# A spectral layer and two MLP layers on one core: rounding of weights in five steps, the mix's split ahead of the threshold, first inverse results in other PSUM banks

## Chip, core, metric

The kernel runs on one core of a Trainium2 chip. The metric is the device time of one launch in microseconds, lower is better. Engines: PE is TensorE, DVE is VectorE, ACT is ScalarE, POOL is GpSimd, SP is the SyncE queue that issues most DMAs.

## What is computed

```python
X = np.fft.rfft(x, axis=1)                   # x: 2 x 3008 x 256
Yr = Xr @ w_r - Xi @ w_i + b_r
Yi = Xr @ w_i + Xi @ w_r + b_i
Yr = np.sign(Yr) * np.maximum(np.abs(Yr) - 0.01, 0.0)   # Yi alike
y = np.fft.irfft(Y, n=3008, axis=1)
h = y.reshape(6016, 256) @ w_in1             # 256 x 2048
z = (h / (1 + exp(-h))) @ w_out1             # 2048 x 256
out = leaky(z @ w_in2) @ w_out2              # maximum(0.01 * h, h)
```

## The kernel before, in words

Every float32 product is made of three passes over parts: a number is split into a high part `hi` (rounded to the format fp32r by a conversion) and a low part `lo` (the difference). So each result that is to be multiplied again costs a copy on ACT (`hi`) and a subtraction on DVE or POOL (`lo`).

The program is one long list in a manual schedule: each engine runs its instructions in the order in which the Python code issues them. It has four stretches. The first transform of length 47 comes first (until about 34 us; `pa`, L276). Then comes the **spectrum**: 48 items, one per frequency row and batch. Then the inverse transform of length 47 (`inverse`, `px`, L424) and the first MLP layer start, interleaved, and the second layer follows.

An item j passes through eight parts. The list `STAGES` (L377) gives their order within one call `spectrum(j)` and the lag of each, so `spectrum(j)` runs `threshold` of item j-3, `split_z` of j-1, `split_y` of j-3, `seed` of j-1, `store` of j-5, `mix` of j, `forward` of j-2 and `backward` of j-4:

- `mix` (L321, PE): six matmuls of 512 columns into `pz`, one of the two banks of `ps_a[0]`.
- `split_z` (L330, L331): ACT copies `pz` to `zh`, DVE subtracts to `zl`. After that the bank is free.
- `seed` (L336, DVE): copies the bias into a bank `py` of `ps_h` (four banks).
- `forward` (L344, PE): six matmuls of 256 columns onto `py`.
- `threshold` (L350, L351): ACT makes `cy` from `py`, DVE then finishes `cy` in place.
- `split_y` (L358, L359): ACT copies `cy` to `yh`; `yl` is subtracted by DVE for even item numbers (so in `spectrum(j)` with odd j) and by POOL for the others.
- `backward` (L367, PE): three matmuls of 256 columns into `pb`, one of the two banks of `ps_a[1]`.
- `store` (L373, L374): ACT copies `pb` to `bo`, SP sends it to memory.

Behind these, `split_dm` splits the transform table of item j+1 (`dmh` by ACT or POOL in turn, L238; `dml` by POOL, L239), and `load_dm` loads that of j+4. In the first 28 items a table serves two items.

Behind each `spectrum(j)` stands `fifth_w(i)`, with i = j % 5 for the first 28 items and (j - 28) % 3 after that. It rounds the first layer's weights piece by piece for later use. `begin` makes `wc` and `wm` on ACT (L138, L140), then two DVE instructions on `wm` (L143, L145); `scale` is one DVE instruction (L150); `around` is an addition on POOL (L157), and with it goes the load of a further piece by SP (L131); `split` is a copy on ACT (L164) and a subtraction on POOL (L165). Splits in this stretch stop at 16 pieces. Before the change, i = 0 or 3 splits one piece and begins another, i = 1 or 4 scales, i = 2 or 4 adds and loads. Inside the MLP layers `step_w` goes on with the rest.

At the end of the loop two groups of the inverse transform are made, with two tiles `px` each (h = 0 and 1): both of the first group, then `spectrum(48)`, then both of the second, then `spectrum(49)`. Each `px` is split by ACT (`xhi`, L431) and DVE (`xlo`, L432). Before the change, h = 0 takes a bank of `ps_a[0]`, h = 1 one of `ps_h`. `spectrum(50)` to `spectrum(52)` run between the first matmuls of the MLP (`ph`, L520, in `ps_h`).

Of the kernel before, what the change touches and what calls it, by code (L numbers as in the profile page):

```python
# [76 lines left out]
def spectral_mlp_kernel(ctx, tc, x, w_r, w_i, b_r, b_i, w_in1, w_out1, w_in2, w_out2, da, ea, dm, out):  # L77
# [3 lines left out]
    def pool(name, bufs, stack=ctx, **kw):  # L81
        return stack.enter_context(tc.tile_pool(name=name, bufs=bufs, **kw))
# [4 lines left out]
    ps_h = pool("ps_h", 4, space=bass.MemoryType.PSUM)  # L87
    ps_a = [pool(f"ps_a{i}", 2, space=bass.MemoryType.PSUM) for i in range(2)]
# [20 lines left out]
    def weight_pieces(win, wout, in_dst, out_dst, n_dst, first=0):  # L109

        win, wout = win.bitcast(U32), wout.bitcast(U32)
        pieces = []
        for q in range(NF // 2 + 1):
            new = []
            if q < NF // 2:
                for d in range(2):
                    new.append((win[d * 128:(d + 1) * 128, q * 512:(q + 1) * 512], lambda d=d, q=q: [w[:, d, q % 4 * 256:][:, :256] for w in in_dst(q // 4)]))  # L120
            if q:
                for f in (2 * q - 2, 2 * q - 1):
                    new.append((wout[f * 128:(f + 1) * 128, :], lambda f=f: [w[:, f % HALF * D:][:, :D] for w in out_dst(f // HALF)]))
            pieces += new[2:] + new[:2] if q == 4 else new
        loaded, begun, scaled, rounded, made = [], [], [], [], []

        def load():
            if pieces:
                src, dst = pieces.pop(0)
                raw = raws[0].tile([128, 512], F32, tag="wraw", name="wraw", bufs=4 if raws[1:] else 2).bitcast(U32)  # L130
                nc.sync.dma_start(out=raw, in_=src)  # L131
                loaded.append((raw.rearrange("p (e w) -> p e w", w=2), dst))

        def begin():
            raw, dst = loaded.pop(0)
            m = stage.tile([128, 256], U32, tag="wm", name="wm", bufs=2)
            c = stage.tile([128, 256], F32, tag="wc", name="wc", bufs=4).bitcast(U32)
            nc.scalar.activation(out=c, in_=raw[:, :, 0], func=ACTF.Copy, scale=2.0 ** -29)  # L138

            nc.scalar.activation(out=m.bitcast(F32), in_=raw[:, :, 1].bitcast(F32), func=ACTF.Copy, scale=2.0 ** -112)  # L140
            yield

            nc.vector.tensor_scalar(out=m.bitcast(F32), in0=m.bitcast(F32), scalar1=MAG, scalar2=-MAG, op0=ALU.min, op1=ALU.max)  # L143
            yield
            nc.vector.tensor_scalar(out=m, in0=m, scalar1=3, scalar2=0x7FFFFFFF, op0=ALU.logical_shift_left, op1=ALU.bitwise_and)  # L145
            begun.append((raw, m, c, dst))

        def scale():
            raw, m, c, dst = begun.pop(0)
            nc.vector.scalar_tensor_tensor(out=m, in0=raw[:, :, 1], scalar=0x80000000, in1=m, op0=ALU.bitwise_and, op1=ALU.bitwise_or)  # L150
            yield
            scaled.append((m, c, dst))

        def around(add):
            m, c, dst = scaled.pop(0)
            r = dst()[0].bitcast(U32) if n_dst == 1 else c
            add.tensor_tensor(out=r, in0=c, in1=m, op=ALU.add)  # L157
            rounded.append((c.bitcast(F32), dst))

        def split():  # L160
            c, dst = rounded.pop(0)
            if n_dst == 2:
                hi, lo = dst()
                nc.scalar.copy(hi, c)  # L164
                nc.gpsimd.tensor_tensor(out=lo, in0=c, in1=hi.bitcast(F32), op=ALU.subtract)  # L165
            made.append(1)

        def step():

            if scaled:  # L170
                around(nc.gpsimd)
            parts = [p() for p, ready in ((scale, begun), (begin, loaded and len(begun) < 2)) if ready]
            done = len(rounded)
            while parts:
                for p in list(parts):
                    if next(p, parts) is parts:
                        parts.remove(p)
            for _ in range(done):
                split()
            if scaled:  # L180
                around(nc.gpsimd)
            load()

        def fifth(i):

            if i in (0, 3):
                if rounded and len(made) < first:
                    split()
                if loaded and not begun:
                    list(begin())  # L190
            elif i in (1, 4) and begun:
                list(scale())
            if i in (2, 4) and scaled:
                around(nc.gpsimd)
                load()

        def until(n):
            while len(made) < min(n, 2 * NF):
                step()

        return load, step, fifth, until

    raws = [stage]
    load_w, step_w, fifth_w, until_w = weight_pieces(
        w_in1, w_out1, lambda k: [w_in[k][p] for p in parts], lambda k: [w_out[k][p] for p in parts], 2, NF)

# [167 lines left out]
        nc.sync.dma_start(out=scr[4 * k:4 * k + 4, b], in_=bo)  # L374


    STAGES = [(threshold, 3), (split_z, 1), (split_y, 3), (seed, 1), (store, 5), (mix, 0), (forward, 2), (backward, 4)]  # L377

    def spectrum(j):
        for part, lag in STAGES:  # L380
            if 0 <= j - lag < len(items):
                part(j - lag)
        split_dm(j + 1)
        load_dm(j + 4)
# [4 lines left out]
    def load_b():  # L389
        if groups:  # L390
            g, n = groups.pop(0)
            b, p = divmod(g, R2 // 2)
            bt = btp.tile([NJ, NG, D], F32, tag="bt", name="bt")
            nc.sync.dma_start(out=bt[:, :n], in_=scr[:, b, p:p + n, :])
            bts.append((g, n, bt))
# [21 lines left out]
    def inverse(h, c):  # L417

        g, n, bt = bts[0]

        at_, tag = (ps_a[1], "acc") if c in (1, 2) else (ps_a[0], "acc") if c == h == 0 else (ps_h, "h")
        px = at_.tile([128, 512], F32, tag=tag, name="px")
        for s in range(n):
            nc.tensor.matmul(px[:, s * PAIR:(s + 1) * PAIR], lhsT=bt[:, s, h * 128:(h + 1) * 128],  # L424
                             rhs=ea_sb, start=True, stop=True, skip_group_check=True)
        t0, t1 = g * PAIR, (g + n) * PAIR
        cut = min(t1, t0 + RING - at(t0))
        for a, b in ((t0, cut), (cut, t1)):
            if a < b:
                hi, lo = (r[:, h, at(a):at(a) + b - a] for r in ring)  # L430
                nc.scalar.copy(hi, px[:, a - t0:b - t0])  # L431
                nc.vector.tensor_tensor(out=lo, in0=px[:, a - t0:b - t0], in1=hi.bitcast(F32), op=ALU.subtract)  # L432
        if h == 1:
            bts.pop(0)
            load_b()
# [13 lines left out]
    made = [0]  # L449

    def ahead(layer, c):

        if layer == 2:
            return [lambda: load_x2(c), None] + [lambda h=h: split_x2(c, h) for h in range(2)]
        steps = []
        while made[0] < sum(CHUNKS[c]):
            made[0] += sizes.pop(0) * PAIR
            steps += [lambda h=h: inverse(h, c) for h in range(2)]
        return steps
# [220 lines left out]
    for i in range(len(pairs) + 2):  # L680
# [70 lines left out]
        if k <= i <= NF:  # L751
            split_w()
            if i < NF:
                sums_w1(i - k)
        elif i < tail:
            if i == NF + 1:
                for home in homes:
                    m_in.append(home.tile([128, DFF], F32, tag="hold0", name="m_in").rearrange("p (d c) -> p d c", d=2))
                    m_out.append(home.tile([128, DFF], F32, tag="hold1", name="m_out"))
                _, step_w, _, _ = weight_pieces(w_in2, w_out2, lambda k: [m_in[k]], lambda k: [m_out[k]], 1)  # L760
            if i > NF and i % 2 == 0:
                step_w()
        else:
            split_w()
            if i - tail in IN_AT:
                next_in(IN_AT.index(i - tail))
            if i - tail in SUMS_AT:
                sums_w2(SUMS_AT.index(i - tail))
# [27 lines left out]
```

## Time and profile before

| | |
|---|---|
| median of 3 runs | 1165.65 us (1165.25 to 1167.86) |
| the profiled execution, whole | 1165.78 us |
| its span, first to last instruction | 1164.0 us |
| PE busy | 1154.2 us (99%) |
| DVE, ACT, POOL busy | 711.3 (61%), 764.3 (66%), 592.0 us (51%) |
| mean granted clock of PE | 1.000 of full speed |

The span is 1.78 us shorter than the execution. Times in the rows are microseconds from the start of the span unless marked ns; a row of the timeline gives start, duration, engine, line, operation, output and inputs, and in brackets the idle time before it with what ended it. Instructions of one engine overlap a little, so the distance from start to start is less than the duration. PE's float32 matmuls are recorded as two each.

### The profile page before, as it was taken

The page shows a single profiled execution, that of the slowest core. Times are in us where ns is not written, and L with a number is a line of the kernel's source. Part 1 is how long each engine was busy: PE and PEld are TensorE (multiplying, and loading weights), DVE is VectorE, ACT ScalarE, POOL GpSimd, SP SyncE. Part 2 cuts the span into 40 slices and gives each one's busy share as a digit, 9 for nine tenths or more (in the row PEclk, how much of TensorE's full clock was granted, in tenths as well). Part 3 has the DMA queues.
Part 4 walks back from the last instruction along what each step waited for, and adds up shares of the span by engine and source line. Part 5 has one row for each costly group of instructions (what it writes and reads, how often), then busy time and mean ns, then how long its engine had stood idle before and what let it go on. Part 6 is the DMA issues. An engine that isn't in the chain of part 4 may idle for free.

```text
span 1164.0 us, 19838 instructions
## 1 busy us (share of the span) xinstructions
PE 1154.2 (99%) x7290; PEld 1047.5 (90%) x7290; DVE 711.3 (61%) x1333; ACT 764.3 (66%) x1551; POOL 592.0 (51%) x649
## 2 busy tenths in 40 slices
PE   9999999999999999999999999999999999999998
PEld 9888888889999999999999999999999999999998
DVE  4788866455666666666665677555455555555553
ACT  4687777566666666666665777566566666566564
POOL 0566745644445445444445666554555455455532
PEclk9999999999999999999999999999999999999999
DMA  9444543101112111111110110011011011101100
GB/s 224 130 133 138 144 140 111 32 28 33 43 42 66 51 42 60 50 37 57 38 37 10 37 32 14 24 37 37 1 37 37 1 37 37 37 1 37 33 1 32
DMA packets 36177, 61.72 MB, mean 53 GB/s; under 512 B 3952, under 2 KB 16080, under 8 KB 36080
## 3 DMA queue, kind: packets, MB, share of 16 engines
q1 hardware_dynamic: 35792, 60.28, 17.6%
q8 instruction: 57, 0.93, 0.4%
q14 instruction: 40, 0.33, 0.1%
q10 hardware_dynamic: 288, 0.18, 0.1%
HBM read 41.83 MB, written 18.61 MB: 52 GB/s over the span
## 4 chain that ended last, share of the span: by engine, by line
PE 94%; ACT 2%; DVE 2%; POOL 1%; issue 1%; DMA 1%; SPq 0%; POOLq 0%; DVEq 0%; ACTq 0%
PE ph L520 44%; PE acc L589 40%; PE pz L321 3%; PE px L424 2%; PE pa L276 2%; PE py L344 2%; PE pb L367 1%; DVE wm L143 1%; POOL dml L239 1%; DVE cy L351 0%; DMA xt<-in_x_dram 0%; DVE zl L331 0%; ACT wm L140 0%; ACT wc L138 0%; ACT bo L373 0%
## 5 line engine op out<-in xcount | busy, mean ns | idle before, releaser
L544 DVE TENSOR_TENSOR lb<-u,hb 128x768 fp32r<-128x768 f32 (+1 forms) x176 | 170.5, 969 | 344.8 <-ACT hb L582 344.6
L544 POOL TENSOR_TENSOR la<-u,ha 128x512 fp32r<-128x512 f32 (+1 forms) x176 | 225.6, 1283 | 265.2 <-ACT ha L582 265.2
L520 PE MATMUL ph<-xhi,winlo 128*128 128x512 f32 (+1 forms) x768 | 236.6, 389 | 0.0
L520 PE MATMUL ph<-xhi,winhi 128*128 128x512 f32 (+1 forms) x768 | 232.4, 383 | 0.0
L520 PE MATMUL ph<-xlo,winhi 128*128 128x512 f32 (+1 forms) x768 | 231.2, 381 | 0.0
L520 PEld LDWEIGHTS ph<-xlo,winhi 128*128 128x128 f32 x768 | 143.5, 188 | 28.8
L520 PEld LDWEIGHTS ph<-xhi,winhi 128*128 128x128 f32 x768 | 143.5, 187 | 26.4
L582 ACT CAST hb<-u 128x768 fp32r<-128x768 f32 (+1 forms) x176 | 140.5, 798 | 5.2 <-DVE u L570 4.2
L589 PE MATMUL acc<-lb,whi 128*128 128x256 f32 (+1 forms) x496 | 137.6, 277 | 0.0
L589 PE MATMUL acc<-hb,wlo 128*128 128x256 f32 (+1 forms) x496 | 137.4, 277 | 0.0
L589 PE MATMUL acc<-hb,whi 128*128 128x256 f32 (+1 forms) x496 | 137.2, 277 | 0.0
L539 ACT ACTIVATE ph<-ph 128x512 f32<-128x512 f32 (+1 forms) x112 | 64.5, 576 | 110.7 <-PE ph L520 110.7
L556 POOL TENSOR_TENSOR u<-u 128x256 f32<-128x256 f32 x160 | 128.1, 801 | 8.1 <-ACT u L539 3.3
L541 ACT ACTIVATE ph<-ph 128x512 f32<-128x512 f32 (+1 forms) x96 | 55.0, 573 | 105.1 <-PE ph L520 104.9
L582 ACT CAST ha<-u 128x512 fp32r<-128x512 f32 (+1 forms) x176 | 109.9, 624 | 18.1 <-POOL u L556 18.1
L520 PEld LDWEIGHTS ph<-xhi,winlo 128*128 128x128 f32 x768 | 119.6, 188 | 2.2
L544 DVE TENSOR_TENSOR l<-ph,h 128x512 fp32r<-128x512 f32 (+1 forms) x176 | 117.4, 667 | 0.0
L563 DVE TENSOR_TENSOR u<-ph,u 128x512 f32<-128x512 f32 x160 | 109.2, 683 | 6.3 <-POOL u L556 6.3
L582 ACT CAST h<-ph 128x512 fp32r<-128x512 f32 (+1 forms) x176 | 102.3, 581 | 0.0
L589 PE MATMUL acc<-la,whi 128*128 128x256 f32 (+1 forms) x352 | 99.0, 281 | 0.0
L589 PE MATMUL acc<-ha,whi 128*128 128x256 f32 (+1 forms) x352 | 99.0, 281 | 0.0
L589 PE MATMUL acc<-ha,wlo 128*128 128x256 f32 (+1 forms) x352 | 98.7, 280 | 0.0
(121 smaller groups left out, 2526.9 us busy)
## 6 DMA issues: line engine op xcount, KB each, us to landing
wraw<-in_moe_w_in_dram SPq DMA_DIRECT2D x32, 256.0 KB
wraw<-in_moe_w_out_dram SPq DMA_DIRECT2D x32, 256.0 KB
scr<-bo SPq DMA_DIRECT2D x48, 128.0 KB
scr<-x2o SPq DMA_DIRECT2D x22, 256.0 KB
x2i<-scr SPq DMA_DIRECT2D x22, 256.0 KB
out_dram<-x2o SPq DMA_DIRECT2D x22, 256.0 KB
dmr<-in_dm_dram SPq DMA_DIRECT2D x34, 160.0 KB
bt<-scr SPq DMA_DIRECT2D x14, 384.0 KB
```

The source lines that it names most:

```text
L276: nc.tensor.matmul(pa[h][:, s * 128:(s + 1) * 128], lhsT=xt[c][:, s, h * 128:(h + 1) * 128], rhs=da_sb, start=True, stop=True, skip_group_ ...
L321: nc.tensor.matmul(turned(pz), lhsT=u[:, h, :], rhs=turned(v[:, h].rearrange("p g e -> p (g e)")), start=(n == 0), stop=(n == len(terms) - 1))
L344: nc.tensor.matmul(turned(py), lhsT=u, rhs=turned(v), start=False, stop=(n == len(terms) - 1), skip_group_check=True)
L424: nc.tensor.matmul(px[:, s * PAIR:(s + 1) * PAIR], lhsT=bt[:, s, h * 128:(h + 1) * 128], rhs=ea_sb, start=True, stop=True, skip_group_chec ...
L520: nc.tensor.matmul(turned(ph), lhsT=u[:, h, f % HALF * 128:][:, :128], rhs=turned(v[:, h, :]), start=(i == 0), stop=(i == len(terms) - 1))
L539: nc.scalar.activation(out=out, in_=ph, func=ACTF.Silu)
L541: nc.scalar.activation(out=out, in_=ph, func=ACTF.Prelu, alpha=0.01)
L544: eng.tensor_tensor(out=lo, in0=src, in1=hi.bitcast(F32), op=ALU.subtract)
L556: nc.gpsimd.tensor_tensor(out=blk(1), in0=blk(0), in1=blk(2), op=ALU.subtract)
L563: nc.vector.tensor_tensor(out=v[:, 3:5], in0=b22, in1=v[:, 0:2], op=ALU.subtract)
L582: nc.scalar.copy(hi, src)
L589: nc.tensor.matmul(turned(dst), lhsT=u, rhs=turned(v), start=(begin and self.p == 0 and i == 0), stop=(end and self.p == NF // 2 - 1 and i ...
```

## The change

Three edits. `fifth` now takes every weight through five calls, one step per item: ACT's half of `begin`; the two DVE instructions of `begin`; `scale`; `around` with the load; `split`. Begins still come at i = 0 and 3. `STAGES` has `split_z` ahead of `threshold`. In `inverse`, the h = 1 tiles of chunk 0 take a bank of `ps_a[1]` in place of `ps_h`.

```diff
-        loaded, begun, scaled, rounded, made = [], [], [], [], []
+        loaded, opened, begun, scaled, rounded, made = [], [], [], [], [], []
...
         def step():
+            while opened:
+                list(opened.pop(0))
...
         def fifth(i):
 
-            if i in (0, 3):
-                if rounded and len(made) < first:
-                    split()
-                if loaded and not begun:
-                    list(begin())
-            elif i in (1, 4) and begun:
-                list(scale())
-            if i in (2, 4) and scaled:
+            if rounded and len(made) < first:
+                split()
+            if scaled:
                 around(nc.gpsimd)
                 load()
+            if begun:
+                list(scale())
+            if opened:
+                list(opened.pop(0))
+            if i in (0, 3) and loaded:
+                opened.append(begin())
+                next(opened[-1])
...
-    STAGES = [(threshold, 3), (split_z, 1), (split_y, 3), (seed, 1), (store, 5), (mix, 0), (forward, 2), (backward, 4)]
+    STAGES = [(split_z, 1), (threshold, 3), (split_y, 3), (seed, 1), (store, 5), (mix, 0), (forward, 2), (backward, 4)]
...
-        at_, tag = (ps_a[1], "acc") if c in (1, 2) else (ps_a[0], "acc") if c == h == 0 else (ps_h, "h")
+        at_, tag = (ps_a[1], "acc") if c in (1, 2) else (ps_a[h], "acc") if c == 0 else (ps_h, "h")
```

## Rows read from the trace of the kernel before

**Rows 1.** Busy time by stretch: length, then PE, PEld, DVE, ACT, POOL, clock, DMA, GB/s
```profile
130.00:140.00 10.00, 8.88 (x57) 7.79 (x56) 8.62 (x19) 7.30 (x21) 6.53 (x9) 1.00 0.51 150
160.20:260.00 99.80, 99.80 (x471) 83.55 (x470) 52.94 (x121) 67.47 (x164) 52.29 (x75) 1.00 0.23 68
```

**Rows 2.** Waits of the whole span, in front of L321: us in total, times, longest
```profile
PEld pz L321 <- PE pb L367: 6.0, 11, 0.9
PE pz L321 <- DVE zl L331: 4.1, 9, 0.8
```

**Rows 3.** Timeline of PE: the starts of four mixes
```profile
45.65 0.68 PE L321 MATMUL pz<-wmlo,ahi 128*128 128x512 f32 x2 [0.55 <-DVE zl L331]
...
65.15 0.62 PE L321 MATMUL pz<-wmlo,ahi 128*128 128x512 f32 x2
...
67.54 0.62 PE L321 MATMUL pz<-wmlo,ahi 128*128 128x512 f32 x2
...
152.22 0.62 PE L321 MATMUL pz<-wmlo,ahi 128*128 128x512 f32 x2
```

**Rows 4.** The chain of waits around one gap: start, us, what
```profile
144.91 0.36 ACT wm L140
...
145.29 0.70 DVE wm L143
...
146.64 0.61 DVE zl L331
```

**Rows 5.** Timeline of ACT, one item
```profile
118.56 0.58 ACT L330 CAST zh<-pz 128x512 fp32r<-128x512 f32 x1
119.15 0.41 ACT L358 CAST yh<-cy 128x256 fp32r<-128x256 f32 x1
119.46 0.37 ACT L373 COPY bo<-pb 128x256 f32<-128x256 f32 x1
119.73 0.41 ACT L164 CAST wouthi<-wc 128x256 fp32r<-128x256 f32 x1
120.03 0.45 ACT L138 ACTIVATE wc<-wraw 128x256 uint32<-128x256 uint32 x1
120.39 0.44 ACT L140 ACTIVATE wm<-wraw 128x256 f32<-128x256 f32 x1
```

**Rows 6.** Timeline of DVE, the same item
```profile
118.69 0.42 DVE L351 SCALAR_TENSOR_TENSOR cy<-py,cy 128x256 f32<-128x256 f32 x1 [0.21 <-ACT cy L350]
119.17 0.69 DVE L331 TENSOR_TENSOR zl<-pz,zh 128x512 fp32r<-128x512 f32 x1
119.77 0.42 DVE L336 COPY py<-bias 128x256 f32<-128x256 f32 x1
```

**Rows 7.** Timeline of ACT: the first item's yh
```profile
41.63 0.41 ACT L358 CAST yh<-cy 128x256 fp32r<-128x256 f32 x1
```

**Rows 8.** Timeline of ACT and PE at the end of the spectrum
```profile
152.51 0.58 ACT L330 CAST zh<-pz 128x512 fp32r<-128x512 f32 x1
...
159.09 0.47 PE L344 MATMUL py<-zh,dml 128*128 128x256 f32 x2 [0.64 <-ACT xhi L431]
...
160.19 0.60 PE L520 MATMUL ph<-xhi,winlo 128*128 128x512 f32 x2
```

**Rows 9.** Groups by line, 45 to 155 us: busy us, mean ns | idle before
```profile
L143 DVE TENSOR_SCALAR wm<-wm 128x256 f32<-128x256 f32 x16 | 8.7, 541 | 10.2 <-ACT wm L140 10.2
...
L145 DVE TENSOR_SCALAR wm<-wm 128x256 uint32<-128x256 uint32 x16 | 7.7, 478 | 0.5
```

**Rows 10.** Line 143 over the whole span: shortest, median and longest in ns
```profile
L143 DVE TENSOR_SCALAR wm<-wm x64: 279/292/929, 35.7 to 613.1; 128x256 f32<-128x256 f32 x64
```

**Rows 11.** Timeline of POOL and DVE at one L143
```profile
105.22 0.87 POOL L239 TENSOR_TENSOR dml<-dmr,dmh 128x320 fp32r<-128x320 f32 x1
...
105.31 0.93 DVE L143 TENSOR_SCALAR wm<-wm 128x256 f32<-128x256 f32 x1 [0.75 <-ACT wm L140]
```

**Rows 12.** The chain of waits: one group of inverse matmuls
```profile
170.55 0.86 PE px L424 x8
```

## Prediction

> **What bounds the kernel now.** I read the busy times by stretch first: from 160.2 us on, TensorE (PE) is busy for all of its time, and the rows show no gap to win or to fill there [rows 1]. So whatever the change does to the spectrum (34 to 160 us) reaches the end of the program unchanged, in either direction. Next, the waits: in the spectrum PE waits for one thing, the two banks of the mix's result `pz`. The 6.0 us at the weight load and the 4.1 us at the matmul are the same gap in front of L321, put down now to the last PE work and now to `zl` [rows 2]. The mix of item j needs the bank of item j-2, which `split_z` frees with `zl`. Third, PE's order of time: undisturbed, the mixes of two items start 67.54 - 65.15 = 2.39 us apart; item 5 starts at 45.65 and item 47 at 152.22, which is 106.57 us for 42 items, 2.54 us each [rows 3]. So the gaps cost 106.57 - 42 x 2.39 = 6.2 us, and no more than that can be won in this stretch. Fourth, the chain of waits says where a gap is made: ScalarE (ACT) finishes the weight's `wm`, VectorE (DVE) has stood waiting for it with `zl` queued behind, and runs L143 before `zl` [rows 4]. The five-step rounding takes exactly this wait away: L143 and L145 then work on a `wm` that ACT made one item earlier.
>
> **The change, part by part.**
>
> *Rounding.* The same instructions are issued for each weight. Begins stay at the same items (0, 3, 5, 8, ... 25, then 28, 31, ... 46: 18 of them); the two DVE steps, the scaling, the addition and the split come 1, 2, 3 and 4 items later. Sixteen weights are split by the end either way, and a seventeenth stands rounded; the eighteenth is one step behind, which the first step inside the first layer takes up, at a VectorE instruction of half a microsecond beside a full PE: nothing. If PE caught up with that, it would wait for that one instruction. The load that goes with each addition is issued by SP one item later at most; it is three weights ahead of its use, over five items or 12 us, so I cost it at nothing; without that lead ACT's queue would stop at its begin. GpSimd (POOL) has room, 6.53 of 10 us busy in the worst stretch [rows 1], and its addition still has an item before ACT's split asks for it.
>
> *Split of the mix first.* This is the expensive part. The rows of one item show ACT's order as `cy`, `zh`, `yh`, `bo`, then the weight's work [rows 5], and DVE's as `cy`, `zl`, `py` [rows 6]. `yh` needs DVE's half of the threshold (L351), and today DVE does that while ACT converts `zh`: `cy` from 118.69 to 119.11, `yh` at 119.15. After the change ACT issues `zh`, `cy`, `yh`, and DVE `zl`, `cy`. From the start of `zh`: `zl` starts 119.17 - 118.56 = 0.61 later, DVE is free for `cy` another 119.77 - 119.17 = 0.60 later, `cy` takes 0.42, and `yh` follows 0.04 behind [rows 5, 6]: 1.67 us, against 0.59 from `zh` to `yh` in this item today [rows 5]. In between ACT has only `cy` to do and stands idle for the rest, with `bo`, `dmh` and all weight work queued behind `yh`. With `yh` to `bo` 0.31 and `bo` to the next instruction 0.27, an item without extras costs ACT 2.25 us.
>
> The extras, from the same rows: `hi` of a split weight 0.30, `wc` and `wm` 0.36 and about 0.35 (0.71 a begin), and `dmh` of the same size, taken as 0.36. Between items 3 and 47 there are 17 begins (12.1 us), 16 splits (4.8) and 16 `dmh` on ACT (5.8); items 3 and 4 have no `bo` (-0.5). Sum: 45 x 2.25 + 12.1 + 4.8 + 5.8 - 0.5 = 123.4 us, or 2.74 an item, above PE's 2.39. So ACT takes PE's place as the bound, and PE and POOL follow with about an item in hand.
>
> Start: `yh` of item 0 begins at 41.63 [rows 7] after a wait for data that stays, so the count begins at 41.63 - 1.67 = 39.96 and ACT ends item 47 at 163.3; its `zh` of that item starts at 161.1. Today it starts at 152.51 [rows 8]. **First term: +8.5 us.**
>
> *DVE late for `zl`.* When `zl` is late, `yh` and ACT are late by as much. On items with odd j, DVE also has `yl`, which waits for `yh`: from the start of `zl` it is free after 1.06 + 0.44 + 0.33 + 0.33 = 2.16 (instructions overlap by 0.09, as `zl` shows), and the next `zl` may start after 2.25 plus ACT's extras. L143 and L145 take 0.54 and 0.48 on average [rows 9], 0.93 with overlap. They overrun by 0.84 less the extras on items 9, 11, 19, 21, 29, 35 and 41: 0.53 + 0.48 + 0.17 + 0.84 + 3 x 0.17 = 2.5; the scaling adds some 0.2. **Second term: +2.7 us.** With 0.28 each (the shortest [rows 10]) it is 0.7. What stretches them is POOL: one L143 took 0.93 while POOL's `dml` ran from 105.22 to 106.09 [rows 11]. If L143 and L145 each waited for a whole such instruction (0.28 + 0.87, 2.3 a weight), the odd items lose 12 and the even ones, which have 1.0 more in hand, 9: 21 us. Those are the ends; I take the mean, since before, too, they ran among POOL's instructions. The Trainium skill states the stronger form (page "SBUF — State Buffer", section "SBUF: two separate sides"): VectorE and GpSimd share a port pair that is locked for a whole instruction, and the loser blocks fully. By it the second term would be anything up to that upper end, as often as the two meet; the trace agrees where they met, and its mean says they meet for part of the time.
>
> *First inverse results.* `px` of h = 1 moves from the four banks of `ps_h` to the two of `ps_a[1]`, between the `pb` tiles. So `px` needs the bank of `pb` 42, and `pb` 44 that of `pb` 43, whose reader `bo` 43 stands in ACT's queue behind `px`'s own conversion, `zh` 47, `cy` and the waiting `yh`. By the same spacings, in us after the `zh` at 161.1: second `px` starts at 2.4 (after `bo` 42) and ends at 3.3 (0.86 for eight matmuls [rows 12]); its `xhi`, taken between `yh` and `zh`, ends at 3.9; `zh` 47, `zl`, `cy`, `yh`, `bo` 43 bring 6.2; `pb` 44 and two `px` bring 7.5, the next `xhi` 7.9, `cy` 46 to `yh` to `bo` 44 another 1.7, `pb` 45 10.0. Then comes the first `ph`. Today it comes 160.19 - 152.51 = 7.7 after that `zh` [rows 8]. **Third term: +2.3 us**; without the move I get 6.4, so this part alone could also give -1.3; a second missed bank would make it +4. The 0.64 us that PE waits there today [rows 8] is within the difference.
>
> **Sum:** 8.5 + 2.7 + 2.3 = +13.5. The profiled execution took 1165.78 us, 0.13 above the median of the runs; 1165.78 + 13.5 = **1179.3 us**.
>
> **Rivals.**
> 1. *PE sets the pace* (faster). The wait behind `wm` was all that held `zl`, and leading with `zh` frees banks earlier: 6.2 us of gaps and the 0.64 go, 1158.9 us. For it: rows 2 and 4 name just this. Against it: ACT then must do an item in 2.39 with 0.50 of extras, so `yh` may start at most 2.39 - 0.58 - 0.50 = 1.31 after `zh`; the rows add up to 1.67. Chance 0.08.
> 2. *A draw.* If `yh` starts 1.46 after `zh`, ACT's item is 2.54, today's mean: about 1165.8. It needs a fifth of a microsecond less in each hand-over than any row shows. Chance 0.06.
> 3. *POOL blocks DVE* (slower still). L143, L145 meet POOL almost always: between half and all of the 21 us in place of 2.7, 1187 to 1198, about 1190. Decides from 1.15 us each; the rows have 0.54 and 0.48. Chance 0.11.
> 4. *The clock.* In a stretch where PE was busy for 8.88 of 10 us the granted clock stayed 1.00 [rows 1]; after the change PE would be busy 2.39 of 2.8, 8.5 of 10. If it fell to the lower level, 1.2 GHz, PE's item would be 4.78, and 45 items would cost 45 x (4.78 - 2.8) = 89 us more, near 1268. The page "TensorE: Matmul & The Clock Gate" of the Trainium skill (section "A second HAM failure mode: psum-queue depth-cycling") tells of a kernel whose PE idles shortly but often between groups of matmuls and swings between the two levels, paying each time; the trace, with gaps up to 0.9 us [rows 2], shows none of that. Chance 0.01.
>
> **How the numbers follow.** My forecast has the remaining 0.74. 0.2%, or 2.3 us, is about what a measurement of this kernel can tell from no change. Faster 0.08 and a part of the draw, 0.09; same 0.05; slower 0.86. The first term alone, with 0.7 for a late `zl` and the gain of 1.3 at the inverse, gives 1173.7; `yh` a tenth of a microsecond earlier in 40 items would take some 4 us off, so the range begins at 1170. It ends at the middle of rival 3, 1190: it holds nearly all of the forecast and half of rival 3, some 0.78.
>
> **What would show it.** In the changed profile ACT's `yh` should wait for DVE's `cy` in nearly every item, some 0.8 us each and 35 us in all; DVE should no longer wait for `wm` in the loop; mixes should start about 2.8 us apart, with PE's wait before L321 far over 10 us; `pb` or `px` should wait for `bo` near the first `px`. I am wrong if the mixes start 2.4 apart, if `yh` starts less than 1.5 after `zh`, or if the granted clock falls in the spectrum.

## The result and the profile after

The changed kernel takes 1180.75 us (median of 4 runs, 1180.2 to 1181.15) against 1166.09 us before (4 runs): a ratio of 1.0123, 95% interval 1.0106 to 1.0141. It is 14.7 us slower. The profiled execution took 1180.57 us, its span 1178.8 us.

Busy time by stretch of the kernel after (columns as in [rows 1]; lines below L122 have moved by up to 4, so `zl` is L335, `cy` L354 and L355, `yh` L362, `bo` L377):

```profile
130.00:140.00 10.00, 9.31 (x51) 7.54 (x51) 6.80 (x16) 7.24 (x20) 6.61 (x10) 1.00 0.43 123
175.00:275.00 100.00, 100.00 (x472) 83.67 (x471) 52.90 (x122) 67.79 (x164) 52.42 (x75) 1.00 0.22 67
```

From the first `ph` on PE is full, as before [rows 1], and the clock stays at 1.00. So the whole loss lies ahead of the first `ph`. That stands at 174.90 us now and stood at 160.19 [rows 8]: 14.7 us later, against 14.8 us in the span.

The waits between 45 and 165 us of the kernel after (who waited for whom: us in total, times, longest):

```profile
ACT yh L362 <- DVE cy L355: 35.0, 42, 1.4
...
DVE zl L335 <- ACT zh L334: 20.3, 21, 1.6
...
PEld pz L325 <- DVE zl L335: 10.6, 22, 0.6
...
PE pz L325 <- DVE zl L335: 6.0, 18, 0.4
```

ACT waits at `yh` in all 42 items, 0.83 us each. VectorE's wait for `wm` has left this stretch. The same stretch in the timeline of ACT shows two items:

```profile
160.44 0.59 ACT L334 CAST zh<-pz 128x512 fp32r<-128x512 f32 x1
160.92 0.49 ACT L354 ACTIVATE cy<-py,lam 128x256 f32<-128x256 f32 x1
162.12 0.41 ACT L362 CAST yh<-cy 128x256 fp32r<-128x256 f32 x1 [0.71 <-DVE cy L355]
162.43 0.37 ACT L377 COPY bo<-pb 128x256 f32<-128x256 f32 x1
162.69 0.46 ACT L242 CAST dmh<-dmr 128x320 fp32r<-128x320 f32 x1
163.06 0.58 ACT L334 CAST zh<-pz 128x512 fp32r<-128x512 f32 x1
...
165.35 0.41 ACT L362 CAST yh<-cy 128x256 fp32r<-128x256 f32 x1 [1.33 <-DVE cy L355]
...
166.63 0.57 ACT L334 CAST zh<-pz 128x512 fp32r<-128x512 f32 x1
```

In the first, `yh` starts 162.12 - 160.44 = 1.68 after `zh` and the item costs 163.06 - 160.44 = 2.62, of which `dmh` is 0.37: 2.25 without it. In the second `yh` starts 2.29 after `zh`. The timelines of VectorE and then of GpSimd say why:

```profile
162.56 0.59 DVE L363 TENSOR_TENSOR yl<-cy,yh 128x256 fp32r<-128x256 f32 x1 [0.47 <-ACT yh L362]
163.08 0.41 DVE L340 COPY py<-bias 128x256 f32<-128x256 f32 x1
163.41 0.98 DVE L150 SCALAR_TENSOR_TENSOR wm<-wraw,wm 128x256 uint32<-128x256 uint32 x1
164.31 0.68 DVE L335 TENSOR_TENSOR zl<-pz,zh 128x512 fp32r<-128x512 f32 x1
...
163.23 0.87 POOL L243 TENSOR_TENSOR dml<-dmr,dmh 128x320 fp32r<-128x320 f32 x1 [0.36 <-ACT dmh L242]
```

VectorE waits 0.47 for `yh`, then does `yl`, `py` and the weight's L150. L150 takes 0.98 us beside GpSimd's `dml`, which ends at 164.10, and `zl` starts 1.25 after `zh` in place of 0.61.

### The profile page after: what moved, and what is told of

It is laid out like the page before. It is cut to its first block, busy times and chain, and to the rows that moved or that the text cites. A ratio compares the mean times of both kernels' runs of the same rounds, so it can differ in the third digit from the quotient of the medians.

```text
span 1178.8 us, 19820 instructions
## 1 busy us (share of the span) xinstructions
PE 1164.4 (99%) x7290; PEld 1047.8 (89%) x7290; DVE 709.0 (60%) x1333; ACT 762.3 (65%) x1551; POOL 589.5 (50%) x649
## 4 chain that ended last, share of the span: by engine, by line
PE 88%; DVE 6%; ACT 4%; issue 1%; POOL 0%; DMA 0%; ACTq 0%; DVEq 0%; POOLq 0%
PE ph L524 44%; PE acc L593 39%; PE px L428 2%; PE pa L280 2%; DVE zl L335 2%; DVE cy L355 1%; ACT zh L334 1%; ACT bo L377 1%; DVE wm L145 1%; ACT yh L362 1%; DVE yl L363 1%; ACT wc L138 0%; DVE py L340 0%; ACT wm L140 0%; PE warm L268 0%
```

## Experiments

Ratios are to the kernel before, run beside it on the same chip. Its median moved between 1165.99 and 1167.60 us from one set of runs to the next, so kernels of different sets are compared by their ratios; 0.001 is 1.2 us. "Late" below is the distance from the start of `zh` to the start of `zl`, as far as it goes beyond 0.61 us, added over the 45 items of `spectrum(3)` to `spectrum(47)`; the loop is the time between the `zh` of these two calls. Both are worked out from the timelines. The kernel after has a loop of 126.7 us and 6.2 us late; the kernel before a loop of 111.5 and 10.8 us late.

### One part at a time

*e1: the changed kernel with the old order of stages.*

```diff
-    STAGES = [(split_z, 1), (threshold, 3), (split_y, 3), (seed, 1), (store, 5), (mix, 0), (forward, 2), (backward, 4)]
+    STAGES = [(threshold, 3), (split_z, 1), (split_y, 3), (seed, 1), (store, 5), (mix, 0), (forward, 2), (backward, 4)]
```

> The changed kernel with the order of the stages put back (threshold ahead of split_z); five-step rounding and the new banks stay. Theory (ACT stands idle between zh and yh because DVE does zl before cy): the loss goes and the 6 us of gaps that the rounding made go too; yh starts about 1.0 us after ACT's cy, mixes about 2.4 to 2.45 us apart, 1159 to 1163 us. Rival (the rounding in five steps or the banks make the loss): stays above 1174 us.

Measured: 1162.99 us, ratio 0.9974 (0.9964 to 0.9985); the loop is 108.7 us. *The order is worth 17.4 us* beside the other two edits (1.0123 - 0.9974).

*e2: the kernel before with the new order only* (the diff above, reversed, on the kernel before).

> The kernel before with only the order of the stages changed (split_z first). Theory: the order alone makes the loss; yh waits about 0.7 us or more for DVE's cy in every item, ACT's item stays at 2.24 us plus the weight work, 1176 to 1182 us. Rival (it needs the five-step rounding beside it): below 1170 us.

Measured: 1183.63 us, ratio 1.0149 (1.0132 to 1.0166), a little above what I had expected: 17.4 us once more. ACT's wait at `yh` is 37.5 us between 45 and 160 us, and VectorE waits 13.3 us for `wm` on top. So the order alone makes the loss, and the two other edits together win some 3 us back (1.0149 against 1.0123). The five steps alone win some 5 us beside the new order: e6 below, which has both and the old banks, stands at 1.0104.

*e3: the kernel before with the five steps only.* The edit is that of `fifth` and `step` in the diff of the change.

> The kernel before with only the rounding in five steps. Theory: DVE no longer waits for wm, most of the 6.2 us of gaps before the mixes go, 1160 to 1163 us. Rival (VectorE is as late for zl for another reason, such as GpSimd): 1165 to 1167 us.

Measured: 1162.65 us, ratio 0.9971 (0.9959 to 0.9982), 3.4 us faster. PE's waits in front of L325 in this kernel, whole span:

```profile
PEld pz L325 <- PE pb L371: 3.0, 5, 0.7
...
PE pz L325 <- DVE zl L335: 2.2, 5, 0.5
```

They were 10.1 us [rows 2] and are 5.2. The other half of the gaps stays: VectorE has no wait for `wm` left between 45 and 150 us, but is late for `zl` with the weight's own instructions. That is 11.0 us in sum, no less than in the kernel before; why it costs PE only half as much is not shown.

*e6: the changed kernel with the old banks.*

```diff
-        at_, tag = (ps_a[1], "acc") if c in (1, 2) else (ps_a[h], "acc") if c == 0 else (ps_h, "h")
+        at_, tag = (ps_a[1], "acc") if c in (1, 2) else (ps_a[0], "acc") if c == h == 0 else (ps_h, "h")
```

> The changed kernel with the first inverse results back in the banks of ps_h. Theory (px and pb share two banks and wait for xlo and bo): the first ph comes 0.5 to 1.9 us sooner after the zh of spectrum(47), 1178.9 to 1180.3 us. Rival (the banks cost nothing): 1180.7 us.

Measured: 1179.22 us, ratio 1.0104 (1.009 to 1.0117), about 2 us less than the change; the intervals overlap. The timelines of ACT and PE in this run:

```profile
166.51 0.58 ACT L334 CAST zh<-pz 128x512 fp32r<-128x512 f32 x1
...
173.58 0.61 PE L524 MATMUL ph<-xhi,winlo 128*128 128x512 f32 x2
```

The first `ph` comes 7.1 us after that `zh`, against 174.90 - 166.63 = 8.3 in the change: 1.2 us for the banks in these two executions, while the loop is the same (126.6). Beside the old order they cost nothing that can be told (e1 against e3, run side by side: 0.3 us, intervals overlapping).

### Is it the idle time behind `cy`?

*e4: store moved into the gap; e7: seed too.* The first new line is e4's, the second e7's.

```diff
-    STAGES = [(split_z, 1), (threshold, 3), (split_y, 3), (seed, 1), (store, 5), (mix, 0), (forward, 2), (backward, 4)]
+    STAGES = [(split_z, 1), (threshold, 3), (store, 5), (split_y, 3), (seed, 1), (mix, 0), (forward, 2), (backward, 4)]
+    STAGES = [(split_z, 1), (threshold, 3), (store, 5), (seed, 1), (split_y, 3), (mix, 0), (forward, 2), (backward, 4)]
```

> The changed kernel with store moved ahead of split_y, so that ACT does bo while it waits for DVE's cy. Theory: yh still starts 1.67 us after zh, and ACT's item is 0.27 us shorter, 1.97 plus the weight work; over 43 items 11 us less, near 1169 us. Rival (ACT's idle time is not what sets the pace): no change, 1180 us.

Measured: 1175.33 us, ratio 1.0079 (1.0064 to 1.0094); the loop is 121.7 us, 5.0 less. The direction is right, the size half of what I had said. Late rises to 12.6 us, and these 6.4 us more are what is missing from the 11 expected. The timeline of VectorE in this run has an odd item in which it never runs dry but for `yh`:

```profile
139.49 0.68 DVE L335 TENSOR_TENSOR zl<-pz,zh 128x512 fp32r<-128x512 f32 x1
...
140.09 0.41 DVE L355 SCALAR_TENSOR_TENSOR cy<-py,cy 128x256 f32<-128x256 f32 x1
...
140.97 0.83 DVE L363 TENSOR_TENSOR yl<-cy,yh 128x256 fp32r<-128x256 f32 x1 [0.47 <-ACT yh L362]
...
141.72 0.41 DVE L340 COPY py<-bias 128x256 f32<-128x256 f32 x1
...
142.06 0.75 DVE L150 SCALAR_TENSOR_TENSOR wm<-wraw,wm 128x256 uint32<-128x256 uint32 x1
...
142.73 0.68 DVE L335 TENSOR_TENSOR zl<-pz,zh 128x512 fp32r<-128x512 f32 x1
```

From `zl` to `zl` is 3.24 us. Where VectorE has `yl`, the loop runs over both engines (`zl`, `cy`, ACT's `yh`, `yl`, `py`, weight, next `zl`), and taking `bo` off ACT's side of it wins nothing. That named the next run:

> As e4_bo_in_gap, with seed ahead of split_y too, so that VectorE copies py while it waits for yh, in place of behind yl. e4 brought half of what was expected. Theory (on odd items VectorE, which waits for yh before yl and copies py behind it, became the bound in e4): VectorE is free 0.33 us sooner on odd items, 22 items, 4 to 7 us less than e4, 1168.5 to 1171.5 us. Rival (py is not in the way, ACT's conversions have another wait): 1175 us as e4.

Measured: 1169.70 us, ratio 1.0022 (1.0012 to 1.0031), 6.6 us less than e4; the loop is 117.0 us, late back at 7.8. So two instructions that the changed order leaves behind the wait, `bo` and `py`, put ahead of it without any other change, take 11.8 us off the 14.3. *So at least half of what the order costs is idle time behind `cy`, on ACT and on VectorE.* It is not all gone in e7:

```profile
ACT yh L362 <- DVE cy L355: 26.4, 42, 1.4
```

That is ACT's wait at `yh` from 45 to 157 us, 35.0 in the change. The old order with the same two ahead of `split_y` is e11 below, at 0.9951. Beside it the new order still costs 8.3 us (1.0022 against 0.9951, the banks included), about half of the 17.4.

### What makes `zl` late beyond that

*e9: the changed kernel without the three VectorE instructions of the rounding.*

```diff
-            nc.vector.tensor_scalar(out=m.bitcast(F32), in0=m.bitcast(F32), scalar1=MAG, scalar2=-MAG, op0=ALU.min, op1=ALU.max)
...
-            nc.vector.tensor_scalar(out=m, in0=m, scalar1=3, scalar2=0x7FFFFFFF, op0=ALU.logical_shift_left, op1=ALU.bitwise_and)
...
-            nc.vector.scalar_tensor_tensor(out=m, in0=raw[:, :, 1], scalar=0x80000000, in1=m, op0=ALU.bitwise_and, op1=ALU.bitwise_or)
```

> The changed kernel without L143, L145 and L150, the three VectorE instructions of the rounding (the weights come out unscaled and unsigned). Theory (what the loop takes above ACT's own sum of instructions and the wait for zl and cy is zl late behind these three): zl starts 0.61 after zh in every item, some 5.5 to 6.2 us less, 1174.5 to 1175.3 us. Rival (yl, which waits for yh on VectorE, makes zl late by itself): 1178 us or above.

Measured: 1175.04 us, ratio 1.0065 (1.0051 to 1.0079), 6.8 us less by the ratios, a little more than expected; the loop is 120.9 us, 5.8 less, and late is 0.4 us. ACT in this run (its lines are as in the kernel before):

```profile
158.61 0.59 ACT L330 CAST zh<-pz 128x512 fp32r<-128x512 f32 x1
...
160.28 0.41 ACT L358 CAST yh<-cy 128x256 fp32r<-128x256 f32 x1 [0.71 <-DVE cy L351]
...
161.54 0.58 ACT L330 CAST zh<-pz 128x512 fp32r<-128x512 f32 x1
```

`yh` starts 1.67 after `zh`, and what is left in the loop is ACT's own sum with the wait for `zl` and `cy`. The three instructions make all of the lateness but 0.4 us.

*e10: GpSimd's `dml` left out* (one low part for all tables).

```diff
+    one_lo = []
...
-            lo = dmp.tile([128, 320], F32R, tag="dml", name="dml")
...
-            nc.gpsimd.tensor_tensor(out=lo, in0=raw, in1=hi.bitcast(F32), op=ALU.subtract)
-            dm_t[j] = hi, lo
+            if not one_lo:
+                one_lo.append(dmp.tile([128, 320], F32R, tag="dml", name="dml", bufs=1))
+                nc.gpsimd.tensor_tensor(out=one_lo[0], in0=raw, in1=hi.bitcast(F32), op=ALU.subtract)
+            dm_t[j] = hi, one_lo[0]
```

> The changed kernel with one low part dml made for the first item and used for all (the low part of the other transform tables is left out). GpSimd does not run dml beside VectorE any more; the instructions of VectorE, ACT and PE are the same. Theory (the three instructions are long because dml holds them up): L150 and L145 get shorter on average (0.53 and 0.78 now), zl is late by 2 to 4 us in sum in place of 6.2, 1176.5 to 1178.5 us. Rival (they are as long by themselves or beside other GpSimd work): 1180 us or above.

Measured: 1179.09 us, ratio 1.0098 (1.0083 to 1.0114), 2.9 us less; late is 3.9 in place of 6.2 us, as expected. The time itself lies just above the range given, beside a kernel before that was 1.5 us slower here than beside the change. The groups by line, 45 to 165 us, first of this run and then of the change (busy us, mean ns):

```profile
L145 DVE TENSOR_SCALAR wm<-wm 128x256 uint32<-128x256 uint32 x16 | 12.0, 749 | 0.6
...
L366 DVE TENSOR_TENSOR yl<-cy,yh 128x256 fp32r<-128x256 f32 x21 | 8.9, 425 | 9.9 <-ACT yh L365 9.9
...
L150 DVE SCALAR_TENSOR_TENSOR wm<-wraw,wm 128x256 uint32<-128x256 uint32 x16 | 7.2, 448 | 0.0
```

```profile
L145 DVE TENSOR_SCALAR wm<-wm 128x256 uint32<-128x256 uint32 x16 | 12.4, 775 | 0.6
...
L363 DVE TENSOR_TENSOR yl<-cy,yh 128x256 fp32r<-128x256 f32 x21 | 10.6, 502 | 9.9 <-ACT yh L362 9.9
...
L150 DVE SCALAR_TENSOR_TENSOR wm<-wraw,wm 128x256 uint32<-128x256 uint32 x16 | 8.5, 529 | 0.0
...
L143 DVE TENSOR_SCALAR wm<-wm 128x256 f32<-128x256 f32 x16 | 5.1, 318 | 0.0
```

`yl` and L150 get shorter without `dml`, L145 hardly. Behind even items it meets GpSimd's `yl` (160.04 to 160.77 in the change, where L145 runs from 160.09 to 160.93), which makes `zl` at most 0.1 late. Behind odd ones another GpSimd instruction takes the place of `dml`. The same L145 in the change and in this run:

```profile
151.88 1.01 POOL L243 TENSOR_TENSOR dml<-dmr,dmh 128x320 fp32r<-128x320 f32 x1 [0.81 <-ACT dmh L242]
152.20 0.85 DVE L145 TENSOR_SCALAR wm<-wm 128x256 uint32<-128x256 uint32 x1
...
150.76 0.73 POOL L165 TENSOR_TENSOR woutlo<-wc,wouthi 128x256 fp32r<-128x256 f32 x1 [2.04 <-ACT wouthi L164]
150.77 0.87 DVE L145 TENSOR_SCALAR wm<-wm 128x256 uint32<-128x256 uint32 x1
```

`zl` behind it, in `spectrum(42)`, is 0.35 and 0.36 late. So leaving `dml` out takes off a good third of the lateness (2.3 of 6.2 us). The rest is other GpSimd work and the instructions' own time: in `spectrum(22)` of the change L143 and L145 run in 0.28 and 0.29 us with nothing of GpSimd beside them, and `zl` is 0.45 late all the same. How much each of the two makes is not parted by these runs.

*e5 and e8: the three instructions only behind even items*, where VectorE has no `yl`; e5 on the changed kernel, e8 on e3.

```diff
-        def fifth(i):
+        def fifth(i, even=True):
...
-            if begun:
+            if begun and even:
...
-            if opened:
+            if opened and even:
...
-        fifth_w(j % 5 if j < 2 * KT else (j - 2 * KT) % 3)
+        fifth_w(j % 5 if j < 2 * KT else (j - 2 * KT) % 3, j % 2 == 0)
```

`wm` has 3 buffers there in place of 2.

> The changed kernel, but the weights' three VectorE instructions (L143, L145, L150) are issued only behind items with even j, where POOL has yl and VectorE is free about 1.1 us before zl is due; wm gets a third buffer. Theory (the part of the loss above ACT's own sum, some 5.9 us in the loop, is zl late behind these instructions on odd items): 3 to 5 us less, 1176 to 1178 us, and the longest items (3.5 us and more) go. Rival (GpSimd holds VectorE back wherever they stand): no change, 1180 us or above.

> The kernel before with the rounding in five steps and its VectorE instructions only behind items with even j; order of the stages and banks as before. Theory (what is left of the gaps in e3_five_only is VectorE overloaded on odd items, which carry yl): 1 to 2.5 us less than e3, 1160.2 to 1161.7 us. Rival (the gaps left have another cause): 1162.7 us as e3.

Measured: 1181.18 us, ratio 1.012 (1.0106 to 1.0133) for e5, 1163.91 us, ratio 0.9971 (0.9961 to 0.9982) for e8. Nothing is won in either; late is 6.8 and 11.5 us. The idea of free even items falls: in some items two weights now meet and all three instructions stand together, and behind even items it is GpSimd's `yl` or `dml` that runs beside them. In e5 L143 took 657 ns on average (318 in the change), L145 635 (775) and L150 414 (529); their sum rose from 1.62 to 1.71 us.

### A better version

*e11: e3 with store and seed ahead of split_y*, threshold still first.

```diff
-    STAGES = [(threshold, 3), (split_z, 1), (split_y, 3), (seed, 1), (store, 5), (mix, 0), (forward, 2), (backward, 4)]
+    STAGES = [(threshold, 3), (split_z, 1), (store, 5), (seed, 1), (split_y, 3), (mix, 0), (forward, 2), (backward, 4)]
```

> The kernel before with the rounding in five steps, and in its old order with store and seed ahead of split_y, so that ACT and VectorE have bo and py to do while yh and yl wait. Theory (in e3_five_only ACT still waits 15 us for cy, part of it on the path): 1 to 2 us less than e3, 1160.6 to 1161.7 us. Rival (that wait is covered by PE there): 1162.7 us as e3, or later where bo holds up yh.

Measured: 1161.62 us, ratio 0.9951 (0.9938 to 0.9963), against 0.9971 for e3; the intervals overlap a little, so a gain over e3 is likely and not shown. It is the fastest of all, 5.7 us below the kernel before by the ratio; its loop is 107.6 us, 108.6 in e3.

## Why the prediction was right, and where its sizes were off

Predicted: slower, 1179.3 us, in a range of 1170 to 1190; measured 1180.75. The mechanism was the one named, and the three terms can be read off one by one, against the `zh` at 152.51 and the first `ph` 7.7 us behind it [rows 8]. The loop is taken from the `zh` of `spectrum(3)` in the change and in e9:

```profile
39.94 0.59 ACT L334 CAST zh<-pz 128x512 fp32r<-128x512 f32 x1 [1.10 <-PE pz L325]
...
40.62 0.59 ACT L330 CAST zh<-pz 128x512 fp32r<-128x512 f32 x1 [1.08 <-PE pz L321]
```

All of e9 begins 0.68 later (its first `yh` at 42.30, 41.62 in the change), so its loop, 161.54 - 40.62 = 120.92, is counted from 39.94, where the prediction had 39.96: without lateness the change's `zh` of `spectrum(47)` would stand at 160.86.

| term | predicted | measured | from |
|---|---|---|---|
| ACT's own sum, `yh` 1.67 behind `zh` | +8.5 | +8.35 | 160.86 against 152.51 |
| DVE late for `zl` | +2.7 | +5.77 | 166.63 in the change against 160.86 |
| first inverse results | +2.3 | +0.59 | 8.27 in the change, 7.68 before |

The sum came nearer (13.5 against 14.7) than the second and third terms did, since one was 3.1 too small and the other 1.7 too large: that part is luck.

- **First term: right.** From four rows of one item [rows 5, 6] the distance from `zh` to `yh` came out at 1.67 us; it is 1.65 to 1.69 wherever `zl` is in time, and an item without extras takes 2.25. ACT's wait of 35 us at `yh` is the one forecast. e2 shows that the order alone does it, e4 and e7 that two instructions in the wait take 11.8 us of it back.
- **Second term: mis-sized by half.** The step "L143 and L145 take 0.54 and 0.48 on average, 0.93 with overlap" kept its sum (0.32 + 0.78 = 1.09), and `zl` was late behind the seven items named; behind these two instructions it was late by some 3.5 us in all, in place of 2.5. What failed is "the scaling adds some 0.2": behind L150 it was late by 2.5 us (0.57 in `spectrum(18)`, 0.64 in three others). L150 ran into `dml` on odd items of the last stretch and, with the `yl` of 0.59 ahead of it (0.42 or 0.43 in most items), made `zl` 0.64 late at the item shown above. I had spread such meetings by their average. But once ACT sets the pace, `dml` starts when ACT's `dmh` ends and L150 when `yl` and `py` are done, both at a fixed distance from `zh`, so they meet on every turn of the last stretch: `zl` starts 1.25 after `zh` in `spectrum(34)`, `(40)` and `(46)` alike. The Trainium skill (page "SBUF — State Buffer", section "SBUF: two separate sides") states an exclusive lock between GpSimd and a VectorE instruction with two inputs in SBUF, as L150 has, or in a two-port mode: whichever starts first holds it for its whole length. The trace agrees roughly where two instructions met: L150 took 0.98 and ended 0.29 after `dml`, where a wait for all of `dml` would end it some 0.41 after (L150's time at 39.94 and 105.89, with nothing of GpSimd beside it). How often they meet only the trace tells, and without `dml` (e10) `zl` is in time in all three.
- **Third term: too large.** The step "`px` needs the bank of `pb` 42, and `pb` 44 that of `pb` 43" failed in its second half. PE in the change:

```profile
171.30 0.38 PE L371 MATMUL pb<-yh,dml 128*128 128x256 f32 x1 [0.43 <-DVE xlo L436]
...
172.97 0.68 PE L428 MATMUL px<-ea_sb,bt 96*128 96x94 f32 x4 [0.64 <-ACT bo L377]
```

  `pb` 44 waited for `xlo` and began before `bo` 43 (at 172.55), so it took the bank that `px` had just left, and the later `px` waited for `bo` 43. By these waits the two banks do not go in turn: the one whose last reader stands earlier in the program was given out first. `pb` 45 (174.44) stands behind an `xlo` too, which ends at 174.38, and not behind `bo` 44, which comes at 175.18, after the first `ph`. So the prediction's step "`cy` 46 to `yh` to `bo` 44 another 1.7" is not on the path: its 10.0 less 1.7 is the 8.3 measured. Without the move I had 6.4, and e6 gives 7.1.
- **Rival 1** was right about its mechanism and wrong about its weight: the five steps do take VectorE's wait for `wm` away, but alone they win 3.4 us (e3), not 6.2 and 0.64; VectorE stays late for `zl` with the weight's instructions themselves. **Rival 2** asked for `yh` 1.46 after `zh`; no item has that. **Rival 3** asked for 1.15 us for each of L143 and L145; they took 1.09 together. **Rival 4**: the granted clock stayed at 1.00, with PE's waits short (0.6 at most in front of L325) and frequent. PE was busy for 9.31 of the 10 us from 130 on, more than the 8.5 that the rival reckoned with.

By one way of taking the edits apart, -3.4 (five steps, e3) + 17.4 (order, e1) + 0.3 (banks, e1 against e3) = +14.3, the ratio 1.0123. This sum closes by the way it is made and is no check. The other way gives +17.4 (order, e2), -5.2 (five steps, e6 against e2) and +2.2 (banks, against e6): the order costs the same both ways, the two small parts differ by no more than their intervals allow.

## What to carry to other kernels

Where two in-order engines hand one value back and forth, look at what each issues between the hand-overs: an order that puts a longer instruction in front of the second hand-over on one engine leaves the other idle there, with all its later work queued behind, even if the moved instruction itself starts sooner. Add up the busiest engine's own spacings with that idle time in, and compare with the pace of the engine that bounds today; here that sum, 8.5 us, was right to 0.2. And when a loop gets a new pacemaker, meetings of two engines' instructions no longer average out: place them in one period and look which of them fall together.

## What I had not expected of the hardware

That a VectorE instruction beside GpSimd's is stretched as regularly as the rows show: L145 had a mean of 775 ns over 16 in the change (478 before [rows 9]) while L143, right ahead of it, fell to 318 (541 before). The pair costs about the same, 1.09 and 1.02; which of the two pays depends here on which one runs beside a GpSimd instruction.

Nor does VectorE always pay. Where L150 began first in the change, `dml` was the longer one:

```profile
53.36 0.42 DVE L150 SCALAR_TENSOR_TENSOR wm<-wraw,wm 128x256 uint32<-128x256 uint32 x1
53.37 1.15 POOL L243 TENSOR_TENSOR dml<-dmr,dmh 128x320 fp32r<-128x320 f32 x1 [1.48 <-ACT dmh L242]
```

The same happens at 76.70 and 110.99; where `dml` began 0.18 or 0.19 earlier (128.18, 145.70, 163.23), it took 0.87 and L150 0.95 to 0.98.
